# Attention over 256-key ranges with float32 scores and two query tiles per bank

## The chip, the cores and the metric

The kernel runs as one program on one core of a Trainium2 chip. The metric is the device time of one execution in microseconds, given as the median of several runs. The core has a matrix engine (TensorE, PE in the profile, with its weight loads listed as PEld), three engines for everything else (VectorE or DVE, ScalarE or ACT, GpSimd or POOL) and a queue engine (SyncE or SP) that issues most transfers. TensorE writes to PSUM, eight banks of 512 float32 columns by 128 partitions; VectorE and ScalarE read it, GpSimd doesn't.

## The reference, cut to what matters

The attention of 2 batches, 8 heads, 768 positions and 64 channels a head is followed by a mixing over the sequence, a two-layer channel mixing and a gated channel mixing. Only the attention is changed. A query sees the 8 global keys at the start and the 96 keys up to its own; the bias is the distance times a slope of the head.

```python
scores = scale * np.matmul(q, k.transpose(0, 1, 3, 2))
rel = pos[:, None] - pos[None, :]
is_global = pos[None, :] < int(n_global)                 # 8
is_local = (rel >= 0) & (rel < int(n_local))             # 96
dist = np.where(is_global & ~is_local, float(n_local), np.abs(rel))
scores = scores - slopes[:, None, None] * dist
scores = np.where(is_global | is_local, scores, -1e9)
a = np.exp(scores - scores.max(-1, keepdims=True))
attn = np.matmul(a / (a.sum(-1, keepdims=True) + 1e-9), v)
```

What follows (U and V of rank 32, then w_ch1, w_ch2, then w_k, w_v, w_r) takes the attention's output as `yp`. The weights arrive as 64-bit words and are turned into pairs of float32r parts by VectorE, ScalarE and GpSimd in the background (`conv`, lines 454 to 472).

## The kernel before, in words

**Head pairs and slots.** The 16 heads are handled as 8 pairs (`PRS`), the two heads of a pair on partitions 0 to 63 and 64 to 127. Each pair's 768 queries are 6 tiles (`NT`) of 128. `slot(pp)` lists the steps of one slot: scores and normalization of pair pp, transposes and P times V of pair pp - 1, preparation of Q and K of pair pp + 1, loads of pair pp + 2. There are 9 slots. Into some are woven steps of other work: slot 5 has the sequence mixing of batch 0 (`u_steps(0)`), slot 7 a split of its result, slot 8 the first channel products; weight conversions are woven into slots 3 and 7. A framework then schedules all instructions by priority and readiness, so the order on an engine is close to that of the lists but not the same, and each engine works its own list in order. It also puts in the waits between engines.

**One pair.** `qprep` and `kprep` transpose Q and K on TensorE and copy them out of PSUM in two float32r parts: ScalarE writes the high part, VectorE the rest (lines 272, 273, 291, 292). K is laid out as `k0 k1 g k2 k3 g k4 k5`, where `g` are the first 32 keys, copied in by VectorE (line 296), so that each query tile's window is one run of 128 to 288 columns. `score` forms three float32r products for each head and query tile (high by high, high by low, low by high), each head with 64 rows of the array and a bank of its own (line 308). VectorE adds the distance window and takes the row's minimum in one instruction (line 312); ScalarE takes the exponential and the row's sum (line 315). `norm` has GpSimd multiply by the reciprocal of the sum (line 334), and copy the 32 global columns of tiles 2 to 5 into `PN`, multiplied too (line 337). `trans` transposes 11 blocks of P for each head on TensorE, four to a bank (line 351); `tglob` transposes `PN` (line 359). These banks are emptied by `ecopy`, which gives every third copy to VectorE (line 512) and the others to ScalarE (line 510). `pv` multiplies with V, each head in a column half of the array, with up to two query tiles in a product (line 374), and adds one product of the global keys for four query tiles and both heads with `VG` (line 367). ScalarE writes the output to `yp` (lines 378 and 380).

**PSUM.** The eight banks have three names: three "a" (scores, later first-layer products), three "t" (all transposes, later half of the second-layer products), two "x" (P times V, later the other half). Line 618 is the first layer of the channel mixing, line 631 the second, lines 717, 733 and 744 the gated one.

Of the kernel before, what the change touches and what calls it, by code (L numbers as in the profile page):

```python
# [23 lines left out]
NGMAX = 32  # L24
# [8 lines left out]
def body(tc, out, q, k, v, n_global, n_local, U, V, w1, w2, mu_k, mu_r, wk, wv, wr):  # L33
    nc = tc.nc
    with ExitStack() as ctx:
# [23 lines left out]
        def constants():  # L59
# [6 lines left out]
            nc.vector.tensor_scalar(out=flag_f[:, 1:2], in0=nl[0:1], scalar1=128.0, scalar2=None, op0=ALU.is_gt)  # L66
# [87 lines left out]
        def attention_windows(pool, actx, cctx, bctx, bank, ecopy):  # L154
            pt_p = pool("ptp", 4, "right", actx)
            st_p = pool("stp", 3, "right", cctx)
            np_p = pool("npp", 11, "right", cctx)
            v_p = pool("vin", 2, "right", cctx)
            pg_p = pool("pgp", 2, "right", cctx)
# [18 lines left out]

            def load_v(pp):
                b, p = PRS[pp]  # L180
                z = st[pp]
                z["v"] = v_p.tile([128, NT, 2, D], F32, tag="vin", name="vin")
                for t in range(2):
                    nc.sync.dma_start(out=z["v"][:, :, t, :],
                                      in_=v[b, 2 * p + t].rearrange("(t p) d -> p t d", p=128))
# [6 lines left out]
            # products of zeros keep the clock of the tensor engine up until the first loads arrive  # L192
# [8 lines left out]
            # distance windows  # L201
            DW = ac.tile([128, 128 + 256 + 288 + 288], F32, name="DW")
            W0, W1, WA, WB = DW[:, 0:128], DW[:, 128:384], DW[:, 384:672], DW[:, 672:960]

            def windows():
                def scratch(dt, n, nm):
                    return np_p.tile([128, 576], dt, tag="P", name=nm)[:, 0:n]
# [15 lines left out]
                nc.vector.copy_predicated(W1, m0.bitcast(U32), relf)  # L223
# [4 lines left out]
                dg = WA[:, 128:160]  # L228
                nc.vector.copy_predicated(dg, gm.bitcast(U32), gd)
                nc.vector.tensor_copy(out=W0, in_=W1[:, 128:256])  # L230
                nc.vector.tensor_copy(out=WA[:, 0:128], in_=W1[:, 0:128])
                nc.vector.tensor_copy(out=WA[:, 160:288], in_=W1[:, 128:256])
                nc.vector.tensor_copy(out=WB[:, 0:32], in_=dg)
                nc.vector.tensor_copy(out=WB[:, 32:288], in_=W1)
                nc.vector.tensor_tensor(out=W0[:, 0:32], in0=W0[:, 0:32], in1=dg, op=ALU.min)
                nc.vector.tensor_tensor(out=W1[:, 0:32], in0=W1[:, 0:32], in1=dg, op=ALU.min)

            VG = gc.tile([64, NPR, 128], F32, name="VG")
            nc.gpsimd.memset(VG, 0.0)

            def load_vg():
                for b in range(B):
                    for t in range(2):
                        nc.sync.dma_start(
                            out=VG[32 * t:32 * (t + 1), b * NP:(b + 1) * NP, 64 * t:64 * (t + 1)],
                            in_=v[b].rearrange("(p t) s d -> t s p d", t=2)[t, 0:32])

            # columns of K: k0 k1 g k2 k3 g k4 k5; the window of a query tile is one run of them
            WIN = {0: (0, 128, W0), 1: (0, 256, W1), 2: (128, 288, WA), 3: (256, 288, WB),
                   4: (416, 288, WA), 5: (544, 288, WB)}  # L250
            # in a window: where the key tile before, the own key tile and the global keys begin
            OFF = {0: (None, 0, None), 1: (0, 128, None), 2: (0, 160, 128), 3: (32, 160, 0),
                   4: (0, 160, 128), 5: (32, 160, 0)}
# [7 lines left out]
            def qprep(pp):  # L261
                b, p = PRS[pp]
                z = st[pp]
                QS = z["QS"] = qk_p.tile([128, 2, S], F32R, tag="QS", name="QS")
                for t0, t1 in HALF:
                    ps = bank("t", "qps")
                    n = (t1 - t0) * 128
                    for i in range(t0, t1):
                        nc.tensor.transpose(ps[:, (i - t0) * 128:(i - t0 + 1) * 128],
                                            z["q"][:, i].rearrange("p h d -> p (h d)"), ident)  # L270
                    cc = slice(t0 * 128, t1 * 128)
                    nc.scalar.activation(out=QS[:, 0, cc], in_=ps[:, 0:n], func=ACTF.Copy, scale=cs[:, p:p + 1])
                    nc.vector.scalar_tensor_tensor(out=QS[:, 1, cc], in0=ps[:, 0:n], scalar=cs[:, p:p + 1],
                                                   in1=QS[:, 0, cc].bitcast(F32), op0=ALU.mult, op1=ALU.subtract)

            def kprep(pp):
# [4 lines left out]
                z["PN"] = pg_p.tile([128, 4, 2, 32], F32, tag="PN", name="PN")  # L281
                KK = z["KK"] = qk_p.tile([128, 2, 3 * 288], F32R, tag="KK", name="KK")
                KKv = KK.rearrange("p l (a n) -> p l a n", a=3)
                for t0, t1 in HALF:
                    ps = bank("t", "kps")
                    a0, a1 = t0 // 2, t1 // 2
                    for i in range(t0, t1):
                        nc.tensor.transpose(ps[:, (i - t0) * 128:(i - t0 + 1) * 128],
                                            z["k"][:, i].rearrange("p h d -> p (h d)"), ident)
                    pv = ps[:, 0:256 * (a1 - a0)].rearrange("p (a n) -> p a n", n=256)  # L290
                    nc.scalar.copy(out=KKv[:, 0, a0:a1, 0:256], in_=pv)
                    nc.vector.tensor_tensor(out=KKv[:, 1, a0:a1, 0:256], in0=pv,
                                            in1=KKv[:, 0, a0:a1, 0:256].bitcast(F32), op=ALU.subtract)
                    if t0 == 0:
                        for a in range(2):
                            nc.vector.tensor_copy(out=KKv[:, :, a, 256:288], in_=KKv[:, :, 0, 0:32].bitcast(F32))

            def score(pp, i):
                b, p = PRS[pp]
                z = st[pp]  # L300
                k0, n, W = WIN[i]
# [16 lines left out]
            def norm(pp, i0, i1):  # L318
# [4 lines left out]
                for i in range(i0, i1):  # L323
                    for t in range(2):
# [3 lines left out]
                        elif i == 1 or i % 2:  # L328
                            o = OFF[i][0]
                            Pl = Pw[:, o:o + 256]  # L330
                        else:
                            Pl = bass.AP(Pw.tensor, Pw.offset, [list(Pw.ap[0]), [160, 2], [1, 128]])
# [476 lines left out]
```

## Time and profile before

| | |
|---|---|
| median of 3 runs | 585.89 us (585.64 to 588.92) |
| profiled execution, span from first to last instruction | 584.2 us, that is 1.7 us less than the median |
| TensorE busy | 564.8 us (97%), 2830 matrix instructions |
| VectorE, ScalarE, GpSimd busy | 336.4, 245.7, 203.1 us |
| last write of attention output (line 380) | starts at 141.8 us |

A profile page gives busy times of each engine, the span in 40 slices, the chain of work that ended last (followed back from the last instruction to what released it), the costliest groups of instructions by line, and the transfers. A group's row reads: line, engine, operation, written tile and read tiles, shape, number of instructions, then busy time in us and mean ns of one, then the engine's idle time just before them and what ended most of it. A matrix product of float32 operands appears as two MATMUL instructions, one of float32r as one. Other views of the same trace show the instructions in order of time, the waits, and busy times in chosen stretches.

### The profile page before, as it was taken

To read this page: it belongs to the slowest core of one execution; us is meant where nothing else is said; L and a number is where in the kernel's file an instruction comes from. 1 tells how busy PE (TensorE), PEld (TensorE's weight loads), DVE (VectorE), ACT (ScalarE), POOL (GpSimd) and SP (SyncE) were. 2 spreads that over 40 slices of the span, in tenths; PEclk is the share of its full clock that TensorE was granted. 3 is DMA by queue.
4 is the path that set the end of the run, shared out by engine and by line. 5 is a ranking of instruction groups with operands and counts; after the bars stand their busy time and mean duration, and the time that the engine had idled before them with its cause. 6 is when DMAs were issued, how large, how long until landed. Compare 5 with 4: busy or idle time off the path is not lost.

```text
span 584.2 us, 7845 instructions
## 1 busy us (share of the span) xinstructions
PE 564.8 (97%) x2830; PEld 442.1 (76%) x2830; DVE 336.4 (58%) x737; ACT 245.7 (42%) x551; POOL 203.1 (35%) x280
## 2 busy tenths in 40 slices
PE   7899999998998999999999999999799999999996
PEld 4666765665786888888888888888688888888886
DVE  5789847896699743737272746569823352344101
ACT  4889856987454413131041332145342144124200
POOL 1577633695053402121040421154452144123300
PEclk9999999999999999999999999999989999999999
DMA  8568821133216320504021224004000000000011
GB/s 159 115 155 232 208 55 29 30 103 119 95 26 204 111 93 0 145 0 145 0 93 52 73 72 145 0 2 144 1 0 20 36 19 0 37 18 20 1 37 41
DMA packets 50031, 41.36 MB, mean 71 GB/s; under 512 B 41472, under 2 KB 41728, under 8 KB 49984
## 3 DMA queue, kind: packets, MB, share of 16 engines
q1 hardware_dynamic: 49696, 40.78, 24.2%
q8 instruction: 24, 0.39, 0.3%
q14 instruction: 23, 0.19, 0.1%
q10 hardware_dynamic: 288, 0.00, 0.0%
HBM read 37.62 MB, written 3.15 MB: 70 GB/s over the span
## 4 chain that ended last, share of the span: by engine, by line
PE 78%; DVE 13%; ACT 3%; issue 2%; POOL 2%; DMA 1%; ACTq 0%; DVEq 0%; POOLq 0%
PE aps L618 19%; PE bps L631 17%; PE pvs L744 11%; PE kps L717 10%; PE prs L733 6%; PE s L308 4%; PE tp L351 3%; DVE cvc L461 3%; PE xb L374 2%; DVE cvc L463 2%; PE gps L551 2%; DVE cvt L459 1%; POOL P L334 1%; ACT P L315 1%; DVE yp L635 1%
## 5 line engine op out<-in xcount | busy, mean ns | idle before, releaser
L618 PE MATMUL aps<-us,w1s 128*128 128x512 f32 x576 | 134.2, 390 | 2.3 <-DVE rs L622 2.3
L631 PE MATMUL bps<-rs,w2s 128*128 128x512 f32 x576 | 133.4, 389 | 0.0
L618 PEld LDWEIGHTS aps<-us,w1s 128*128 128x128 f32 x576 | 107.6, 188 | 26.9 <-DVE rs L622 3.1
L631 PEld LDWEIGHTS bps<-rs,w2s 128*128 128x128 f32 x576 | 108.1, 188 | 22.4
L621 ACT ACTIVATE rs<-aps 128x512 fp32r<-128x512 f32 x48 | 28.1, 595 | 132.6 <-PE aps L618 132.5
L717 PE MATMUL kps<-mix,wk 128*128 128x512 f32 x288 | 67.7, 396 | 3.4 <-DVE kf L722 3.4
L717 PEld LDWEIGHTS kps<-mix,wk 128*128 128x128 f32 x288 | 55.1, 192 | 15.5 <-DVE kf L722 3.9
L334 POOL TENSOR_SCALAR P<-P,sm 128x256 f32<-128x256 f32 (+1 forms) x96 | 48.9, 518 | 43.2 <-DVE sm L322 29.1
L622 DVE SCALAR_TENSOR_TENSOR rs<-aps,rs 128x512 fp32r<-128x512 f32 x48 | 32.9, 687 | 53.3 <-ACT rs L621 53.1
L744 PE MATMUL pvs<-wv,kh 128*128 128x512 f32 (+1 forms) x208 | 61.9, 373 | 0.0
L461 DVE SCALAR_TENSOR_TENSOR cvc<-cvc,cvt 128x512 uint32<-128x512 uint32 (+2 forms) x55 | 49.3, 910 | 10.0 <-ACT cvc L460 9.9
L635 DVE TENSOR_TENSOR yp<-bps,yp 128x512 f32<-128x512 f32 (+1 forms) x64 | 33.9, 550 | 31.2 <-PE bps L631 31.2
L315 ACT ACTIVATE P<-P,nm 128x288 f32<-128x288 f32 (+2 forms) x96 | 48.1, 505 | 6.2 <-DVE nm L312 5.8
L470 POOL TENSOR_TENSOR w2s<-cvc,w2s 128x512 fp32r<-128x512 f32 x16 | 24.7, 1566 | 66.8 <-ACT w2s L468 66.8
L699 POOL TENSOR_SCALAR mixt<-yp,mu 128x512 f32<-128x512 f32 (+1 forms) x32 | 21.6, 681 | 74.8 <-DVE mixf L701 30.3
L460 ACT ACTIVATE cvc<-stg 128x512 f32<-128x512 f32 (+2 forms) x55 | 36.4, 668 | 24.8 <-POOL w1s L470 6.9
L470 POOL TENSOR_TENSOR w1s<-cvc,w1s 128x512 fp32r<-128x512 f32 x16 | 22.8, 1443 | 68.2 <-ACT w1s L468 68.2
L312 DVE CUSTOM_DVE_ANT_0 P<-s,DW 128x288 f32<-128x288 f32 (+2 forms) x96 | 37.3, 417 | 13.1 <-PE s L308 12.7
L463 DVE SCALAR_TENSOR_TENSOR cvc<-stg,cvc 128x512 uint32<-128x512 uint32 (+1 forms) x54 | 43.4, 822 | 0.1
L744 PEld LDWEIGHTS pvs<-wv,kh 128*128 128x128 f32 x208 | 38.1, 188 | 6.9
L724 POOL TENSOR_TENSOR kl<-kf,kh 128x512 fp32r<-128x512 f32 x24 | 31.0, 1290 | 35.1 <-ACT kh L723 35.1
L308 PE MATMUL s<-KK,QS 64*128 64x288 f32 (+2 forms) x288 | 40.7, 323 | 1.4 <-DVE nm L312 1.1
(114 smaller groups left out, 716.6 us busy)
## 6 DMA issues: line engine op xcount, KB each, us to landing
stg<-in_moe_w_ch_dram SPq DMA_DIRECT2D x32, 512.0 KB, 4.3
stg<-in_moe_w_k_dram SPq DMA_DIRECT2D x8, 512.0 KB, 4.4
stg<-in_moe_w_v_dram SPq DMA_DIRECT2D x8, 512.0 KB, 3.8
qin<-in_q_dram SPq DMA_DIRECT2D x16, 192.0 KB, 3.5
kin<-in_k_dram SPq DMA_DIRECT2D x16, 192.0 KB, 3.6
vin<-in_v_dram SPq DMA_DIRECT2D x16, 192.0 KB, 3.3
out_dram<-sg SPq DMA_DIRECT2D x11, 256.0 KB, 2.0
stg<-in_moe_w_r_dram SPq DMA_DIRECT2D x4, 512.0 KB, 3.9
```

The source lines that it names most:

```text
L308: nc.tensor.matmul(sps[t], lhsT=z["QS"][r, lq, qs], rhs=z["KK"][r, lk, k0:k0 + n], start=(x == 0), stop=(x == 2))
L312: nc.vector.tensor_tensor_reduce(out=P[:, t, 0:n], in0=sp, in1=W, scale=2.0 ** -(2 * p + t + 1), scalar=TOP, op0=ALU.add, op1=ALU.min, acc ...
L315: nc.scalar.activation(out=P[:, t, 0:n], in_=P[:, t, 0:n], func=ACTF.Exp, scale=-1.0, bias=z["nm"][:, i, t:t + 1], accum_out=z["sm"][:, i, ...
L334: nc.gpsimd.tensor_scalar(out=Pl, in0=Pl, scalar1=sc, scalar2=1.0, op0=ALU.mult, op1=ALU.mult)
L461: nc.vector.scalar_tensor_tensor(out=c, in0=c, scalar=3, in1=t, op0=ALU.logical_shift_left, op1=ALU.bitwise_or)
L463: nc.vector.scalar_tensor_tensor(out=c if plain is None else plain, in0=Hh, scalar=0x80000000, in1=c, op0=ALU.bitwise_and, op1=ALU.bitwise_or)
L470: nc.gpsimd.tensor_tensor(out=lo, in0=f, in1=hi.bitcast(F32), op=ALU.subtract)
L618: nc.tensor.matmul(ps, lhsT=wsl(("w1", g), lw, kk, f * 128, 128), rhs=us[c][:, lx, kk, :], start=(n == 0), stop=(n == 11))
L631: nc.tensor.matmul(ps, lhsT=wsl(("w2", g), lw, f, o * 128, 128), rhs=r[:, lx, f, :], start=(n == 0), stop=(n == 11))
L635: nc.vector.tensor_tensor(out=ys, in0=ps[:, a:e], in1=ys, op=ALU.add)
L717: nc.tensor.matmul(ps, lhsT=wsl("wk", lw, kk, f * 128, 128), rhs=xk[:, lx, kk, :], start=(n == 0), stop=(n == 11))
L744: nc.tensor.matmul(pv, lhsT=ks[c][lx][:, f, t * 128:(t + 1) * 128], rhs=wsl("wv", lw, f, c0, c1 - c0), start=(n == 0), stop=(n == 23))
```

## The change

- **Key ranges.** K is laid out as six tiles of 160 columns: 128 keys and then the 32 global keys. The window of query tile i > 0 is one run of 256 columns: the last 96 keys of the tile before, the 32 global keys, the own 128 keys. Tile 0 keeps 128 columns. This serves up to 96 local keys (before: 128); beyond it the general path runs, as before.
- **A second copy of V.** `vg` holds for each query tile from 1 on the rows that belong to the first 128 columns of its window: 96 rows of V and the 32 global ones, so P times V needs two products of 128 rows for each tile and head, and no separate product of the global keys. `PN`, `PG`, `VG` and `tglob` go.
- **Scores.** Q and K are no longer split; each head and tile has one float32 product. VectorE's parts of `qprep` and `kprep` go. K leaves PSUM by `ecopy`; GpSimd copies the global columns.
- **Two query tiles per bank.** `score` handles two tiles: columns 0 to 255 and 256 to 511 of one bank for each head. There are four "a" banks and two "t" banks. In `slot` the calls of `score` are 0, 2 and 4 in place of 0 to 5, and `tglob` goes.
- **P times V** runs in blocks of 128 columns, with one "x" bank for tiles 0 and 1 and one for the other four.

The diff, cut to its core:

```diff
-            np_p = pool("npp", 11, "right", cctx)
+            np_p = pool("npp", 12, "right", cctx)
...
             def load_v(pp):
...
+                z["vg"] = v_p.tile([128, NT - 1, 2, D], F32, tag="vgin", name="vgin")
                 for t in range(2):
+                    vh = v[b, 2 * p + t]
+                    nc.sync.dma_start(out=z["v"][:, :, t, :], in_=vh.rearrange("(t p) d -> p t d", p=128))
+                    nc.sync.dma_start(out=z["vg"][0:96, :, t, :],
+                                      in_=vh[32:672].rearrange("(t p) d -> p t d", p=128)[0:96])
+                    g = vh[0:32]
+                    nc.sync.dma_start(out=z["vg"][96:128, :, t, :],
+                                      in_=bass.AP(g.tensor, g.offset, [list(g.ap[0]), [0, NT - 1], list(g.ap[1])]))
...
             def qprep(pp):
-                    nc.scalar.activation(out=QS[:, 0, cc], in_=ps[:, 0:n], func=ACTF.Copy, scale=cs[:, p:p + 1])
-                    nc.vector.scalar_tensor_tensor(out=QS[:, 1, cc], in0=ps[:, 0:n], scalar=cs[:, p:p + 1],
-                                                   in1=QS[:, 0, cc].bitcast(F32), op0=ALU.mult, op1=ALU.subtract)
+                    nc.scalar.activation(out=QS[:, t0 * 128:t1 * 128], in_=ps[:, 0:n], func=ACTF.Copy,
+                                         scale=cs[:, p:p + 1])
             def kprep(pp):
-                    nc.scalar.copy(out=KKv[:, 0, a0:a1, 0:256], in_=pv)
-                    nc.vector.tensor_tensor(out=KKv[:, 1, a0:a1, 0:256], in0=pv,
-                                            in1=KKv[:, 0, a0:a1, 0:256].bitcast(F32), op=ALU.subtract)
+                    ecopy(out=KKv[:, t0:t1, 0:128], in_=pv)
                     if t0 == 0:
-                        for a in range(2):
-                            nc.vector.tensor_copy(out=KKv[:, :, a, 256:288], in_=KKv[:, :, 0, 0:32].bitcast(F32))
+                        nc.gpsimd.tensor_copy(out=KKv[:, 0:NT - 1, 128:KS],
+                                              in_=KKv[:, 0:1, 0:32].to_broadcast([128, NT - 1, 32]))
+            def score(pp, i0):
+                sps = [bank("a", "s") for t in range(2)]
+                for x in range(2):
+                    i = i0 + x
+                    k0, n = (KS * (i - 1) + 32, 256) if i else (0, 128)
+                    for t in range(2):
+                        r = slice(64 * t, 64 * (t + 1))
+                        nc.tensor.matmul(sps[t][:, 256 * x:256 * x + n], lhsT=z["QS"][r, i * 128:(i + 1) * 128],
+                                         rhs=z["KK"][r, k0:k0 + n], start=True, stop=True)
+                for x in range(2):
...
             def norm(pp, i0, i1):
+                        Pl = z["P"][i][:, t, 0:256 if i else 128]
-                        if i >= 2:
-                            o = OFF[i][2]
-                            nc.gpsimd.tensor_scalar(out=z["PN"][:, i - 2, t, :], in0=Pw[:, o:o + 32], scalar1=sc,
-                                                    scalar2=1.0, op0=ALU.mult, op1=ALU.mult)
             def pv(pp, half):
+                X = bank("x", "xa" if half == 0 else "xb")
+                i0, i1 = ((0, 2), (2, NT))[half]
+                for i in range(i0, i1):
+                    for x in (0,) if i == 0 else (2 * i - 1, 2 * i):
+                        for t in range(2):
+                            lhsT = z["vg"][:, i - 1, t, :] if x % 2 else z["v"][:, i, t, :]
+                            nc.tensor.matmul(X[64 * t:64 * (t + 1), c0:c0 + 128], lhsT=lhsT, rhs=z["PT", t][:, x, :],
+                                             start=(x == (0, 3)[half]), stop=(x == (2, 10)[half]))
             def slot(pp):
...
                 add(cur, score, pp, 4)
+                add(cur, norm, pp, 3, 6)
                 add(pre, trans, o, 0, 2)
-                add(cur, score, pp, 5)
-                add(cur, norm, pp, 3, 6)
                 add(pre, trans, o, 1, 2)
...
-                banks = {"a": 3, "t": 3, "x": 2}
+                banks = {"a": 4, "t": 2, "x": 2}
```

More of the change, by code (lines that the diff above doesn't have):

```diff
@@ L227, in windows @@
                 nc.vector.tensor_scalar(out=gd, in0=colf, scalar1=0.0, scalar2=nl, op0=ALU.mult, op1=ALU.add)
-                dg = WA[:, 128:160]
+                dg = W1[:, 96:128]
                 nc.vector.copy_predicated(dg, gm.bitcast(U32), gd)
                 nc.vector.tensor_copy(out=W0, in_=W1[:, 128:256])
[L231 to L234, printed above, removed]
                 nc.vector.tensor_tensor(out=W0[:, 0:32], in0=W0[:, 0:32], in1=dg, op=ALU.min)
[L236 to L253, printed above, removed]
+            KS = 160
             HALF = ((0, 4), (4, 6))
@@ L263, in qprep @@
                 z = st[pp]
-                QS = z["QS"] = qk_p.tile([128, 2, S], F32R, tag="QS", name="QS")
+                QS = z["QS"] = qk_p.tile([128, S], F32, tag="QS", name="QS")
                 for t0, t1 in HALF:
@@ L300, in score @@
                 z = st[pp]
-                k0, n, W = WIN[i]
-                P = z["P"][i] = np_p.tile([128, 2, 288], F32, tag="P", name="P")
-                qs = slice(i * 128, (i + 1) * 128)
-                sps = [bank("a", "s")[:, 0:n] for t in range(2)]
-                for t, x in ((0, 0), (0, 1), (1, 0), (0, 2), (1, 1), (1, 2)):
-                    lq, lk = ((0, 0), (0, 1), (1, 0))[x]
-                    r = slice(64 * t, 64 * (t + 1))
-                    nc.tensor.matmul(sps[t], lhsT=z["QS"][r, lq, qs], rhs=z["KK"][r, lk, k0:k0 + n],
-                                     start=(x == 0), stop=(x == 2))
@@ L348, in trans @@
                 ps = bank("t", "tp").rearrange("p (a n) -> p a n", a=4)
-                for x, (j, i) in enumerate(blks):
-                    o = OFF[i][1] if i == j else OFF[i][0]
-                    nc.tensor.transpose(ps[:, x, :], z["P"][i][:, t, o:o + 128], ident)
+                for x, (i, c) in enumerate(blks):
+                    nc.tensor.transpose(ps[:, x, :], z["P"][i][:, t, c:c + 128], ident)
                 ecopy(out=z["PT", t][:, 4 * g:4 * g + m, :], in_=ps[:, 0:m, :])
-            def tglob(pp):
-                z = st[pp]
-                z["PG"] = pg_p.tile([64, 4, 128], F32, tag="PG", name="PG")
-                ps = bank("t", "tg").rearrange("p (a n) -> p a n", a=4)
-                for x in range(4):
-                    nc.tensor.transpose(ps[0:64, x, :], z["PN"][:, x].rearrange("p h c -> p (h c)"), ident)
-                ecopy(out=z["PG"], in_=ps[0:64])
             def pv(pp, half):
@@ L393, in slot @@
                 add(pre, trans, o, 0, 0)
-                add(cur, score, pp, 1)
                 add(pre, trans, o, 1, 0)
@@ L399, in slot @@
                 add(pre, trans, o, 0, 1)
-                add(cur, score, pp, 3)
                 add(pre, trans, o, 1, 1)
-                add(pre, tglob, o)
                 add(nxt, kprep, pp + 1)
```

77 lines of the change are left out of this document (26 added, 51 removed).

## The prediction

> **What bounds the kernel now.** I read the page first.
>
> ```profile
> span 584.2 us, 7845 instructions
> PE 564.8 (97%) x2830; PEld 442.1 (76%) x2830; DVE 336.4 (58%) x737; ACT 245.7 (42%) x551; POOL 203.1 (35%) x280
> PE 78%; DVE 13%; ACT 3%; issue 2%; POOL 2%; DMA 1%; ACTq 0%; DVEq 0%; POOLq 0%
> ```
>
> The execution profiled has a span of 584.2 us; the median of the runs is 585.89, so 1.7 us lie around it. TensorE is busy 97% and is 78% of the chain that ended last. The change touches only the attention, so the table by stretch comes next, cut where the output rows of a head pair (`yp<-xb`) are written, which ends a slot. A row has the stretch and its length, the busy time and instructions of PE, PEld, DVE, ACT and POOL, the granted clock, the DMA share and GB/s.
>
> ```profile
> 11.00:35.30 24.30, 22.01 (x157) 15.25 (x158) 16.76 (x79) 19.69 (x65) 13.15 (x35) 1.00 0.60 126
> 35.30:48.60 13.30, 12.83 (x107) 9.27 (x106) 12.21 (x44) 12.96 (x40) 7.84 (x17) 1.00 0.81 209
> 48.60:63.00 14.40, 14.11 (x106) 10.02 (x105) 13.50 (x47) 12.25 (x38) 10.59 (x22) 1.00 0.75 206
> 63.00:75.70 12.70, 12.63 (x104) 8.94 (x103) 9.47 (x39) 11.16 (x36) 8.74 (x22) 1.00 0.70 178
> 75.70:102.70 27.00, 27.00 (x158) 15.33 (x159) 17.37 (x49) 17.53 (x48) 9.32 (x24) 1.00 0.20 45
> 102.70:116.20 13.50, 13.40 (x100) 9.08 (x99) 11.52 (x42) 12.19 (x38) 8.86 (x19) 1.00 0.13 30
> 116.20:129.40 13.20, 12.64 (x92) 8.69 (x91) 12.38 (x40) 12.20 (x37) 13.02 (x23) 1.00 0.38 109
> 129.40:142.40 13.00, 12.30 (x83) 9.23 (x82) 8.34 (x11) 8.97 (x19) 10.48 (x15) 1.00 0.27 84
> ```
>
> Each slot is as long as TensorE is busy in it, to 0.7 us. But in the five slots of 12.7 to 14.4 us ScalarE stands between 0.1 us ahead of it and 1.9 behind. So TensorE time saved counts only until ScalarE is the longer one; that sets the sum. (The stretch at 75.7 holds the first half of the mixing too.)
>
> **TensorE, per slot.** The timeline of the slot from 63 us, PE only, start and length first. Matmul lengths hold the pipeline's tail, so I take start to next start.
>
> ```profile
> 63.35 0.62 PE L308 MATMUL s<-KK,QS 64*128 64x256 f32 x6
> 63.91 0.66 PE L351 MATMUL tp<-ident,P 128*128 128x128 f32 x4
> ...
> 65.15 0.67 PE L308 MATMUL s<-KK,QS 64*128 64x288 f32 x6
> 65.75 0.66 PE L351 MATMUL tp<-ident,P 128*128 128x128 f32 x4
> ...
> 67.94 0.39 PE L308 MATMUL s<-KK,QS 64*128 64x288 f32 x1
> 68.26 0.63 PE L359 MATMUL tg<-ident,PN 128*64 128x128 f32 x4
> 68.72 0.82 PE L288 MATMUL kps<-ident,kin 128*128 128x128 f32 x6
> ...
> 71.04 1.02 PE L367 MATMUL xb<-PG,VG 64*128 64x512 f32 x2
> 71.99 0.55 PE L351 MATMUL tp<-ident,P 128*128 128x128 f32 x3
> 72.47 0.87 PE L374 MATMUL xa<-PT,vin 128*64 128x256 f32 x8
> 73.17 1.90 PE L374 MATMUL xb<-PT,vin 128*64 128x128 f32 x20
> 75.00 0.44 PE L542 MATMUL xtp<-ident,yp 128*128 128x128 f32 x2
> ```
>
> *Global keys.* The transposes tg (0.46 us, 68.26 to 68.72) and the product with VG (0.95) go: 1.41 us.
>
> *P times V.* The list shows one float32 product of VG as two MATMULs (x2). The 20 of xb are 12 of 256 columns and 8 of 128: 4096 columns in 1.83 us, 0.45 ns each. VG's two need 0.95 us for 1024 columns, 0.93 ns each. So the two heads of P times V, in two halves of the array, run at once. After the change there are 11 blocks of 128 columns, the same 1408 columns for each head, in 44 MATMULs instead of 28: 44 x 128 x 0.45 = 2.53 us, as now (0.70 + 1.83). Finer pieces: 0 to +0.4 us; I take 0.
>
> *Scores.* Now 6 float32r products per query tile, three for each head: 0.56 us at 256 columns, 0.60 at 288. A tile that finds too few of the three banks "a" is torn: the one product at 67.94 holds TensorE 0.32 us.
>
> ```profile
> L308 PE MATMUL s<-KK,QS 64*128 64x288 f32 (+2 forms) x288 | 40.7, 323 | 1.4 <-DVE nm L312 1.1 <-DVE KK L292 0.3
> ```
>
> 40.7 / 8 = 5.1 us per slot, tails in; less 0.07 for some seven runs, 4.6. After: three calls of two tiles. Float32 at 64 rows in two row halves isn't in the trace. The nearest rows: float32 in column halves runs at once, and so does float32r in row halves: at 0.45 ns per column (134.2 us for 576 of 512 columns in L618, quoted below) 6 x 256 would need 0.70 us in turn and took 0.56 with fill and drain. If the new ones do too, a call is 8 MATMULs of 256 columns at 0.45, 0.92 us, plus 0.21 to fill and drain (0.56 less 3 x 256 x 0.45): 1.13, and 0.90 for the call with tile 0. That is 3.2 us per slot, 1.4 less than now. If they don't, 0.93 ns a column gives 2.1 + 2.1 + 1.6 = 5.8, 1.2 more. I take the first.
>
> The Trainium skill, "TensorE: Matmul & The Clock Gate", section The mechanism, says that MATMULs keep strict order in start and end and only weight loads are pulled ahead. By it the second pass of one head would run beside the first of the other, and each call would end one pass later than I take; the rivals price this from rows.
>
> TensorE thus loses 1.4 + 1.4 = 2.8 us per slot, 22 over eight pairs. That is the ceiling.
>
> **ScalarE, VectorE, GpSimd.** Groups up to 142.4 us:
>
> ```profile
> L315 ACT ACTIVATE P<-P,nm 128x288 f32<-128x288 f32 (+2 forms) x96 | 48.1, 505 | 6.2 <-DVE nm L312 5.8
> L291 ACT CAST KK<-kps 128x512 fp32r<-128x512 f32 (+1 forms) x16 | 7.0, 479 | 1.3 <-PE kps L288 1.1
> L510 ACT COPY PG<-tg 64x512 f32<-64x512 f32 x5 | 2.9, 575 | 0.3 <-PE tg L359 0.3
> L273 DVE SCALAR_TENSOR_TENSOR QS<-qps,cs,QS 128x512 fp32r<-128x512 f32 (+1 forms) x16 | 9.2, 611 | 0.1
> L292 DVE TENSOR_TENSOR KK<-kps,KK 128x512 fp32r<-128x512 f32 (+1 forms) x16 | 8.1, 548 | 0.0
> L296 DVE CAST KK<-KK 128x64 fp32r<-128x64 f32 x16 | 2.4, 190 | 0.0
> L337 POOL TENSOR_SCALAR PN<-P,sm 128x32 f32<-128x32 f32 x64 | 23.5, 367 | 0.0
> ```
>
> ScalarE keeps all 96 exponentials (32 columns fewer in 64 of them, 0.15 us per slot as an estimate), loses a third of the K copies (7.0 / 8 / 3 = 0.29) and PG (2.9 / 8 = 0.36): **0.8 us per slot**, of 11 to 13. VectorE loses (9.2 + 8.1 + 2.4) / 8 = 2.5 us and takes 0.4 of K copies. GpSimd loses 2.9 and gains one copy of 160 columns per pair; nearest row: 367 ns for 32 columns, so 0.37 and somewhat more. That copy stands in GpSimd's queue behind up to three tiles of P multiplies, and the next pair's scores wait for it; K is transposed at 68.72, 6.3 us before the slot's products are done (75.00), which hides it; without that cover up to 2 us a slot.
>
> **Transfers.** A pair issues six loads instead of two; the four of VG go.
>
> ```profile
> vin<-in_v_dram SPq DMA_DIRECT2D x16, 192.0 KB, 3.3
> q1 hardware_dynamic: 49696, 40.78, 24.2%
> ```
>
> 24.2% of 584 us over 49,696 packets is 2.8 ns each over the 16 engines; 1280 more small packets make 3.6 us of transfer per pair. Beside a share of 0.81 that fills the engines in the slots at 35 to 75 us, but V is used a slot after its issue, and Q and K of a pair more than half a slot after theirs: hidden. If not, 1 to 2 us in each of three slots.
>
> **Banks.** "t" goes from 3 to 2 and now holds ten groups a slot (six of P, two Q, two K).
>
> ```profile
> 66.60 0.69 DVE L512 COPY PT<-tp 128x512 f32<-128x512 f32 x1
> 67.34 0.42 PEld L351 LDWEIGHTS tp<-ident,P 128*128 128x128 f32 x4 [0.31 <-DVE PT L512]
> ```
>
> The group at 65.75 holds its bank until 67.29, 1.54 us, and with three banks TensorE already waited 0.31 us for one. Ten groups at 1.6 to 1.8 over two banks are 8 to 9 us of a slot: below ScalarE, but close enough to add waits. Later work uses "t" and "x" in turn:
>
> ```profile
> L618 PE MATMUL aps<-us,w1s 128*128 128x512 f32 x576 | 134.2, 390 | 2.3 <-DVE rs L622 2.3
> L631 PE MATMUL bps<-rs,w2s 128*128 128x512 f32 x576 | 133.4, 389 | 0.0
> ```
>
> A group of 12 takes 2.8 us (134.2 / 48), and a "t" bank returns after three or more groups, so L631 stays without a wait; the fourth "a" bank can win back at most L618's 2.3 us. I take 0 for the rest after 142.4 us and shift it.
>
> **The sum.** A slot after is the larger of TensorE less 2.8 and ScalarE less 0.8, plus 0.7 for two engines of nearly one length (today up to 0.7 over TensorE). At 35.3: 12.2 + 0.7 against 13.3, saves 0.4. At 48.6: 11.5 + 0.7 against 14.4, 2.2. At 63.0: 10.4 + 0.7 against 12.7, 1.6. At 75.7 TensorE stays longest: 24.2 + 0.3 against 27.0, 2.5. At 102.7: 11.4 + 0.7, 1.4. At 116.2: 11.4 + 0.7, 1.1. The last has no scores; tg and VG go, 1.3. From 11 to 35.3 ScalarE is nearly full from 12 us on, 1.6 from it and 0.4 at the end: 2.0. The start loses the low parts of Q and K and four window copies on VectorE but still waits for the limits from memory: 0.5 of a possible 2.5. Sum 13.0: 585.9 - 13.0 = **573 us**.
>
> **Rivals.** *TensorE's whole saving counts* (the order written by the framework fills ScalarE's idle time, 24 of 131 us in the rows above): 22 us and 1 at the start, 563. For it: PE leads the chain; against: ScalarE's 12.96 of 13.30.
> *The row halves don't run at once:* scores +1.2 for 1.4 saved: 0.2 us in each of seven slots, the last slot's 1.3 and the start: 583, no change to measure. Against it: the 0.56 of a 256-column tile.
> *Strict order of MATMULs:* two passes of one head come ahead of the other's, so each call ends a pass (0.24 us) later; 24 calls, 6 us: 579. Against it: the float32r products stand in the code with two of one head in a row, which would give four steps of 0.12 and 0.21, 0.69 us, not 0.56. This is the rule of the Trainium skill's "TensorE: Matmul & The Clock Gate" named above; the trace doesn't bear it out.
> *Slower: the two "t" banks.* Evictions on ScalarE queue behind exponentials of 0.5 us each. Once a group holds its bank over 2.66 us on the mean (10 x 2.66 / 2 = 13.3), the banks set the slot. If each eviction came three exponentials later (3 x 0.505), 3.0 us each, the slot would be 15, +1.7 in seven slots: 598. Against it: 1.54 now, and VectorE, which evicts one in three, loses work.
>
> **How the numbers follow.** Forecast 0.62 (568 to 579); whole saving 0.14; no overlap 0.08; strict order 0.06; banks 0.10, of it half inside 1%. A measurement of this kernel tells about 1%, 5.9 us, from no change. Faster: 0.62 + 0.14 + 0.06 = 0.82, less 0.02 for the forecast's edge: 0.80. Same: 0.08 + 0.05 + 0.02 = 0.15. Slower 0.05. The range takes in the whole saving at 563 and the lack of overlap at 583, with 1 us on either side for V's loads, pieces and banks.
>
> **What would show it.** Right: s falls from 40.7 to about 27 us and x288 to x192; L359, L367, L337, L273, L296 are gone; `yp<-xb` is last written at about 130 us; ScalarE is busy over 90% of the slots and stands in the chain where PE stood; the rest after it keeps its 442 us (584.2 less 142.4). Wrong: s near 45; idle of tp put down to PT copies over 10 us; scores waiting for GpSimd's copy into KK or for DMA; a longer stretch after the attention.

## The result and the profile after

The changed kernel takes **572.08 us** (median of 4 runs, 571.46 to 572.15), against 586.62 us for the kernel before in the same job: ratio 0.973, 95% interval 0.9696 to 0.9763. The profiled execution has a span of 570.2 us, 14.0 less than the 584.2 of before. The prediction was 573.0 in a range of 562 to 584.

The total is right, but its two halves are not where the prediction put them. The last head pair's rows are now written at 132.8 us instead of 142.35, so the attention gave 9.6 us and not 13.0. The rest takes 437.4 us (570.2 less 132.8) instead of 441.8, so 4.4 us came from code that the diff doesn't touch and that the prediction left at zero. The last of these copies on the timelines of before and after (start, length):

```profile
141.76 0.59 ACT L380 COPY yp<-xb 128x512 f32<-128x512 f32 x1
```
```profile
132.20 0.58 ACT L342 COPY yp<-xb 128x512 f32<-128x512 f32 x1
```

The page of the changed kernel: span, share of each engine, the chain that ended last, and the groups of the later products (the line; busy time, mean ns; idle time before them and what ended it).

```profile
span 570.2 us, 7710 instructions
PE 549.4 (96%) x2814; PEld 430.7 (76%) x2814; DVE 318.0 (56%) x688; ACT 238.5 (42%) x540; POOL 184.6 (32%) x223
...
PE 79%; DVE 9%; ACT 4%; POOL 2%; issue 2%; SPq 1%; DMA 1%; POOLq 0%; DVEq 0%
...
L576 PE MATMUL aps<-us,w1s 128*128 128x512 f32 x576 | 135.1, 391 | 0.4 <-DVE rs L580 0.4
...
L675 PE MATMUL kps<-mix,wk 128*128 128x512 f32 x288 | 65.8, 389 | 0.0
```

TensorE is still what bounds the kernel, and ScalarE didn't take its place in the chain. The stretches of the attention, cut again where `yp<-xb` is written (length; busy time and instructions of PE, PEld, DVE, ACT, POOL; granted clock, DMA share, GB/s):

```profile
0.00:30.75 30.75, 24.65 (x173) 15.58 (x174) 16.67 (x95) 20.75 (x68) 12.08 (x34) 1.00 0.77 151
30.75:42.20 11.45, 11.45 (x102) 8.15 (x102) 5.23 (x26) 9.96 (x32) 5.10 (x13) 1.00 0.59 133
42.20:54.70 12.50, 12.11 (x104) 8.28 (x102) 6.84 (x32) 10.05 (x34) 5.95 (x15) 1.00 0.78 185
54.70:68.80 14.10, 12.54 (x105) 9.32 (x104) 9.90 (x39) 11.52 (x38) 7.27 (x15) 1.00 0.49 110
68.80:97.80 29.00, 27.75 (x167) 15.18 (x165) 17.04 (x65) 21.57 (x65) 8.80 (x19) 1.00 0.40 107
97.80:109.70 11.90, 10.39 (x94) 7.40 (x92) 10.44 (x29) 9.36 (x26) 10.54 (x14) 1.00 0.53 150
109.70:120.70 11.00, 9.81 (x86) 6.85 (x87) 9.43 (x32) 10.28 (x32) 7.14 (x9) 1.00 0.79 209
120.70:132.80 12.10, 10.94 (x91) 8.87 (x89) 11.86 (x17) 9.09 (x18) 9.18 (x10) 1.00 0.41 134
```

ScalarE is busy for less time than TensorE in seven of the eight, and for over 90% of the stretch in one of them only, where the prediction expected it of the slots. Against before, the first stretch became 4.5 us shorter and five of the slots 0.9 to 2.2 each, but the slot that ends at 68.8 grew by 1.4 and the one that ends at 97.8 by 2.0.

**Where the other 4.4 us are.** The page of before has, in its list of groups, a row that the prediction never looked at:

```profile
L717 PE MATMUL kps<-mix,wk 128*128 128x512 f32 x288 | 67.7, 396 | 3.4 <-DVE kf L722 3.4
```

That is the gated mixing. From its first product to the first of `prs` the stretch of before, and three pieces of it cut at the steps of the granted clock:

```profile
410.20:437.40 27.20, 23.76 (x98) 19.14 (x98) 14.74 (x21) 11.01 (x19) 13.76 (x11) 0.94 0.00 1
416.41:419.83 3.42, 2.17 (x10) 1.48 (x8) 3.42 (x5) 0.62 (x1) 1.51 (x2) 1.00 0.00 0
419.83:423.24 3.41, 1.22 (x5) 1.04 (x6) 1.04 (x3) 2.24 (x4) 1.81 (x2) 1.00 0.00 0
423.24:426.65 3.41, 3.41 (x9) 2.65 (x9) 1.30 (x2) 1.79 (x4) 2.23 (x3) 0.50 0.00 0
```

and the same stretch of the changed kernel:

```profile
401.10:422.90 21.80, 21.80 (x98) 18.02 (x97) 13.51 (x19) 9.68 (x17) 13.19 (x10) 1.00 0.00 1
```

With three "a" banks TensorE had filled all three and waited 3.44 us for VectorE's `kf`; then the clock stood at 0.50 for 3.41 us, which costs half of these 3.41 us, 1.7, on top. With four banks there is neither: 27.1 us became 21.8, **5.3 us** won. L618's wait of 2.3 us is 0.4 now too (L576 above), another 1.9. Of these 7.2 us some 2.8 are given back elsewhere between 132.8 us and the end, 1.7 of them in longer waits of TensorE in the sequence mixing (L509) and before L589.

### The profile page after: what moved, and what is told of

Same layout as the page of the kernel before. It is cut to its first block, busy times and chain, and to the rows that moved or that the text cites. A ratio compares the mean times of both kernels' runs of the same rounds, so it can differ in the third digit from the quotient of the medians.

```text
span 570.2 us, 7710 instructions
## 1 busy us (share of the span) xinstructions
PE 549.4 (96%) x2814; PEld 430.7 (76%) x2814; DVE 318.0 (56%) x688; ACT 238.5 (42%) x540; POOL 184.6 (32%) x223
## 4 chain that ended last, share of the span: by engine, by line
PE 79%; DVE 9%; ACT 4%; POOL 2%; issue 2%; SPq 1%; DMA 1%; POOLq 0%; DVEq 0%
PE aps L576 19%; PE bps L589 19%; PE pvs L702 12%; PE kps L675 11%; PE prs L691 6%; PE s L292 3%; ACT P L302 2%; PE tp L327 2%; PE gps L509 2%; PE xb L340 2%; POOL P L313 2%; DVE cvc L419 2%; DVE cvc L421 2%; DVE us L547 1%; DVE cvt L417 1%
## 5 line engine op out<-in xcount | busy, mean ns | idle before, releaser
L576 PE MATMUL aps<-us,w1s 128*128 128x512 f32 x576 | 135.1, 391 | 0.4 <-DVE rs L580 0.4
L589 PE MATMUL bps<-rs,w2s 128*128 128x512 f32 x576 | 133.8, 389 | 0.8 <-DVE yp L593 0.8
L576 PEld LDWEIGHTS aps<-us,w1s 128*128 128x128 f32 x576 | 107.5, 188 | 25.2 <-issue 2.5
L589 PEld LDWEIGHTS bps<-rs,w2s 128*128 128x128 f32 x576 | 107.9, 188 | 23.5 <-PE bps L589 1.2
L675 PE MATMUL kps<-mix,wk 128*128 128x512 f32 x288 | 65.8, 389 | 0.0
L313 POOL TENSOR_SCALAR P<-P,sm 128x256 f32<-128x256 f32 (+1 forms) x96 | 50.4, 546 | 35.3 <-DVE sm L309 20.5
L419 DVE SCALAR_TENSOR_TENSOR cvc<-cvc,cvt 128x512 uint32<-128x512 uint32 (+2 forms) x55 | 46.2, 852 | 7.2 <-ACT cvc L418 6.8
L302 ACT ACTIVATE P<-P,nm 128x256 f32<-128x256 f32 (+1 forms) x96 | 46.2, 485 | 8.7 <-DVE nm L299 8.5
L421 DVE SCALAR_TENSOR_TENSOR cvc<-stg,cvc 128x512 uint32<-128x512 uint32 (+1 forms) x54 | 47.1, 892 | 0.1
L299 DVE CUSTOM_DVE_ANT_0 P<-s,DW 128x256 f32<-128x256 f32 (+1 forms) x96 | 34.0, 396 | 18.9 <-PE s L292 18.7
L702 PE MATMUL pvs<-wv,kl 128*128 128x512 f32 (+1 forms) x104 | 38.8, 373 | 0.0
```

The source lines that it names most:

```text
L299: nc.vector.tensor_tensor_reduce(out=P[:, t, 0:n], in0=sps[t][:, 256 * x:256 * x + n], in1=W, scale=2.0 ** -(2 * p + t + 1), scalar=TOP, o ...
L302: nc.scalar.activation(out=P[:, t, 0:n], in_=P[:, t, 0:n], func=ACTF.Exp, scale=-1.0, bias=z["nm"][:, i, t:t + 1], accum_out=z["sm"][:, i, ...
L313: nc.gpsimd.tensor_scalar(out=Pl, in0=Pl, scalar1=z["sm"][:, i, t:t + 1], scalar2=1.0, op0=ALU.mult, op1=ALU.mult)
L419: nc.vector.scalar_tensor_tensor(out=c, in0=c, scalar=3, in1=t, op0=ALU.logical_shift_left, op1=ALU.bitwise_or)
L421: nc.vector.scalar_tensor_tensor(out=c if plain is None else plain, in0=Hh, scalar=0x80000000, in1=c, op0=ALU.bitwise_and, op1=ALU.bitwise_or)
L576: nc.tensor.matmul(ps, lhsT=wsl(("w1", g), lw, kk, f * 128, 128), rhs=us[c][:, lx, kk, :], start=(n == 0), stop=(n == 11))
```

## The experiments

**One part undone: the banks.** Two kernels, each with the other's banks: the changed kernel with three "a" and three "t", and the kernel before with four and two.

```diff
-banks = {"a": 4, "t": 2, "x": 2}     # in the changed kernel
+banks = {"a": 3, "t": 3, "x": 2}
```

> The changed kernel with the banks of before, three "a" and three "t". Theory: the wait for kf returns, 27 us from the first kps<-mix product to the first prs product, 5.3 us more; in the attention three "a" banks tear more score calls of two tiles (TensorE +1 to +4 us) and the third "t" bank takes away the waits of transposes for ScalarE's copies (5 us in all in the waits), so the attention ends within 2 us of 132.8 and the time is 575 to 580. Rival 1 (the banks do nothing later): 570 to 573. Rival 2 (two "t" banks hold the attention back): it ends 4 us earlier.

> The kernel before with four "a" and two "t" banks, nothing else. Theory (a fourth bank carries TensorE over the first products of the gated mixing): the wait of L717 for kf, 3.4 us before, goes and with it the halved clock behind it, so the stretch from the first kps<-mix product to the first prs product falls from 27.1 to 21.8 us, 5.3 less, and the time by 3 to 6 us, since two "t" banks may cost up to 2 in the attention. Rival (the 5.3 us came from the order of the later work having shifted, not from the banks): that stretch stays at 27 us and the time within 2 us of 586.

The changed kernel with the old banks: 581.11 us, ratio to before 0.9896 (0.9847 to 0.9945), so 9 us are lost and the time lies 1 us above the theory's range. The page's row of `kps` and the last stretch have the old wait back; the two stretches ahead of it have the clock halved:

```profile
L675 PE MATMUL kps<-mix,wk 128*128 128x512 f32 x288 | 67.7, 396 | 3.4 <-DVE kf L680 3.4
```
```profile
119.17:126.00 6.83, 5.39 (x16) 4.45 (x17) 2.52 (x6) 1.78 (x4) 2.62 (x3) 0.50 0.45 142
136.24:139.65 3.41, 3.41 (x10) 2.66 (x9) 2.33 (x6) 0.91 (x2) 3.41 (x1) 0.50 0.77 184
403.60:430.70 27.10, 23.70 (x98) 19.08 (x96) 14.64 (x21) 10.92 (x19) 13.74 (x11) 0.94 0.00 1
```

Its attention ended at 131.3, 1.5 us earlier than with two "t" banks although the clock was halved for 6.83 us in it: the new banks do cost the attention something, and pay it back later. Behind the attention the profiled execution is 9.1 us longer: 5.3 in the mixing, 1.9 in L576's waits, some 1.7 of the clock halved at 136.24. The kernel before with the new banks: 599.62 us, ratio 1.0204 (1.0157 to 1.0251), not the 3 to 6 us less that were expected. Its mixing took 21.75 us as foreseen, but the attention ended at 160.2, 17.8 later. Of these, 10.6 lie behind 109.8 us, and this is why (the waits, then the stretch in which nothing ran on TensorE, the one behind it, and the mixing):

```profile
ACT cvc L460 <- POOL w1s L470: 6.8, 1, 6.8
```
```profile
126.70:130.10 3.40, 0.00 (x0) 0.00 (x0) 0.61 (x4) 0.78 (x2) 2.58 (x5) 1.00 0.86 325
130.15:147.21 17.06, 15.84 (x68) 9.60 (x69) 6.57 (x23) 9.55 (x32) 7.37 (x20) 0.50 0.13 43
429.75:451.50 21.75, 21.75 (x97) 18.02 (x96) 13.46 (x19) 9.67 (x17) 13.17 (x10) 1.00 0.00 1
```

ScalarE's next instruction was a weight conversion's copy, and its buffer was held by an earlier conversion whose low part stood in GpSimd's queue. ScalarE, and with it its evictions of "t" banks, stood for 6.8 us; TensorE emptied; the clock then ran at half for 17 us. The other 7.2 us were lost earlier, 0.7 to 2.6 in each stretch. The first of these holds 10.2 us of halved clock; no wait of TensorE between 36 and 110 us is longer than 0.7 us, and the cause stays open. So the new banks help the later stages alone, and whether they help the sum depends on the rest. That the wait for `kf` hangs on the banks is shown by all 14 traces: it is there, 3.39 to 3.44 us long, in the eight kernels with three "a" banks and in none of the six with four.

**One part undone: the scores.** The changed kernel with its Q and K split again and three float32r products; two query tiles in a bank as they are.

```diff
-nc.tensor.matmul(sps[t][...], lhsT=z["QS"][r, ...], rhs=z["KK"][r, ...], start=True, stop=True)
+for t, m in ((0, 0), (0, 1), (1, 0), (0, 2), (1, 1), (1, 2)):   # three products per head, low parts on VectorE
```

> The changed kernel with the scores alone undone: Q and K split again by ScalarE and VectorE and three float32r products for each head and tile; key ranges, second V and two tiles per bank stay. TensorE then streams 3 x 256 columns where the float32 product streams 4 x 256, so a call of two tiles should take 0.87 us instead of 1.06, 24 calls 4.6 us less; VectorE gets 2.2 us a slot more, ScalarE 0.3. Theory that TensorE's length sets the slots: 568 to 570. Theory that copies out of PSUM and the two "t" banks set them (VectorE holds Q's and K's banks 1.1 us longer per pair): 572 to 578. Theory of the change's own words (unsplit products are what pays): 577 or more.

584.65 us, ratio 0.9957 (0.9939 to 0.9976): 12.6 us of the gain are gone, which only the third theory allowed, and the attention ends 13.6 later. The middle slots stayed within 1.3 us of what they were; the start lost 6.4 and the last two 6.9. The first stretch, and two pieces of it with the clock halved:

```profile
0.00:37.10 37.10, 29.43 (x200) 20.99 (x200) 20.49 (x101) 21.57 (x67) 13.24 (x38) 0.82 0.63 130
9.64:16.46 6.82, 6.57 (x40) 5.47 (x42) 2.58 (x12) 3.46 (x12) 0.64 (x2) 0.50 0.69 138
19.88:26.70 6.82, 5.00 (x29) 4.15 (x30) 3.08 (x18) 5.28 (x21) 4.46 (x12) 0.50 0.69 135
```

TensorE or VectorE? The next kernel keeps the float32 scores and lets VectorE compute the low parts all the same.

```diff
+ql = qk_p.tile([128, 512], F32R, tag="QL", name="QL")
+nc.vector.scalar_tensor_tensor(out=ql[:, 0:n], in0=ps[:, 0:n], scalar=cs[:, p:p + 1],
+                               in1=QS[:, cc], op0=ALU.mult, op1=ALU.subtract)   # and the like for K
```

> The changed kernel, scores in float32 as they are, but VectorE still computes the low parts of Q and K as before (they are not used), so that the transposes' banks are held for them too. Theory A, the 12.6 us that the changed kernel loses when its scores go back to three float32r products come from VectorE's 2.2 us a slot and the two banks held longer: 579 to 586. Theory B, they come from TensorE's products: 572 to 576.

578.60 us, ratio 0.9841 (0.9799 to 0.9884), between the two theories: 6.5 of the 12.6 us come back with VectorE's split and the banks held for it. (K's copies all go to ScalarE then, which also shifts the turns in which the engines copy P, so the split doesn't stand quite alone.) It is not the slots that pay but the two ends (stretches, then TensorE's waits in the last one):

```profile
0.00:34.50 34.50, 26.39 (x180) 16.46 (x180) 21.79 (x109) 23.07 (x76) 12.96 (x36) 1.00 0.71 140
122.25:139.10 16.85, 12.31 (x88) 9.26 (x86) 13.89 (x20) 8.70 (x18) 10.41 (x11) 0.90 0.40 127
```
```profile
PE aps L581 <- POOL w1s L433: 1.9, 1, 1.9
PE tp L332 <- POOL P L318: 1.6, 1, 1.6
```

At the start, where little else is there to run, the split stands between Q's and K's transposes and the first scores: 34.5 us instead of 30.75. In the last slot there is no split; there the order has shifted, TensorE waits twice for GpSimd, and 3.4 us of halved clock follow: 16.85 instead of 12.1. The float32r kernel's attention ends another 7.3 us later: 2.7 of it at the start, 2.0 in the next five slots, 2.6 in the last two. There the longer products and the halved clock can't be told apart.

**One part alone: float32 scores in the kernel before**, one product per head and tile, everything else as it was; and the same with the seven early weight conversions one to a slot, beside the kernel before with its conversions so spread, since the first had met the stall shown above.

```diff
-for t, x in ((0, 0), (0, 1), (1, 0), (0, 2), (1, 1), (1, 2)):   # three float32r products
+for t in range(2):                                              # one float32 product
```
```diff
-CONV = {3: 3, 7: 4}
+CONV = {1: 1, 2: 1, 3: 1, 4: 1, 5: 1, 6: 1, 7: 1}
```

> The kernel before with one part of the change alone: Q and K unsplit, the scores as one float32 product per head and query tile (windows of 288, three and three banks, the global products and V's pieces stay as they were). Theory A, the scores are the larger part of the gain whatever else changes: TensorE needs about 0.5 us for a tile instead of 0.60 (-0.7 us a slot) and VectorE loses 2.3 us a slot, so the attention ends 6 to 11 us earlier than 142.4 and the time is 575 to 580. Theory B, float32 scores pay only with two query tiles in a bank: one tile's product of 2 x 288 columns with its fill and drain and the change between float32 and transposes leaves it where it was, 584 to 588.

> The kernel before, the seven conversions of weights that stand in slots 3 and 7 put one to a slot (slots 1 to 7), nothing else: the yardstick for the next runs, in which no copy of a conversion on ScalarE should stand for long behind a conversion's low part that waits in GpSimd's queue, as it did for 5.5 us with float32 scores alone and for 4.8 us with finer pieces alone. Theory A, before had no such stall (1.0 us), so this is its equal: 584 to 588. Theory B, the place of the conversions is worth some us of itself: 578 to 583.

> Float32 scores alone in the kernel before, conversions one to a slot. Theory A, the 6 us by which float32 scores alone were slower than before came from the stall of a conversion and the halved clock behind it, and the scores themselves gain: 5 to 9 us under the run with conversions spread alone, 577 to 582. Theory B, the scores gain only with two tiles to a bank: within 2 us of it.

Alone: 591.77 us, ratio 1.0058 (1.0036 to 1.0081), a little slower and above both expectations. ScalarE had stood for 5.5 us (the waits), TensorE for a whole stretch, and the clock fell:

```profile
ACT cvc L454 <- POOL uv L466: 5.5, 1, 5.5
```
```profile
62.50:65.90 3.40, 0.00 (x0) 0.00 (x0) 0.45 (x1) 0.27 (x1) 3.01 (x7) 1.00 0.49 162
65.92:72.74 6.82, 5.16 (x19) 2.95 (x20) 3.10 (x12) 5.53 (x18) 0.00 (x0) 0.50 0.47 115
```

Spread alone is worth nothing measurable (587.43; 0.9971, 0.9943 to 0.9999). Float32 scores on top of it: 589.01 (1.001, 0.998 to 1.004). That kernel still met a stall of 4.5 us, with the clock halved for 6.83 us behind it, so it isn't clean either, but the 577 to 582 of theory A are far off, and its products show why. The waits of the float32 kernel, then the groups of `s` up to the attention's end, spread alone and with float32 scores, then two runs from the latter's timeline:

```profile
ACT cvc L454 <- POOL w1s L464: 4.5, 1, 4.5
```
```profile
L308 PE MATMUL s<-KK,QS 64*128 64x288 f32 (+2 forms) x288 | 40.0, 321 | 2.2 <-DVE nm L312 1.9 <-DVE KK L292 0.3
```
```profile
L303 PE MATMUL s<-KK,QS 64*128 64x288 f32 (+2 forms) x192 | 42.4, 437 | 1.1 <-ACT KK L289 0.6 <-DVE nm L306 0.5
```
```profile
35.42 0.76 PE L303 MATMUL s<-KK,QS 64*128 64x288 f32 x4
...
39.53 0.75 PE L303 MATMUL s<-KK,QS 64*128 64x288 f32 x2
```

The product of one head (x2) takes as long as those of both (x4), since the second half of the array would have run beside it; 15 of the 50 runs of `s` hold one head alone. And a whole tile isn't cheaper either: from start to next start its four MATMULs hold TensorE for 0.69 us (the middle of 29 such runs), where six float32r products held it for 0.60. In the changed kernel a call of two tiles holds it for 1.06 us, 0.53 a tile of 256 columns. VectorE's relief is there in both float32 kernels (the first head pair's rows are written at 33.25 us instead of 35.44 with the conversions spread), but the slots behind give it back. So the theory that float32 alone is the larger part of the gain fell, as far as two disturbed runs can tell: it pays with two tiles to a bank, not by itself.

**The global keys' way and the pieces.** P times V in pieces of 128 columns in the kernel before; and that with the global keys' own transposes and product left out, with the conversions as they were and spread.

```diff
-runs = ((0, 0, 2), (1, 2, 3), (1, 3, 4), (2, 4, 6), (3, 6, 8), (4, 8, 10), (5, 10, 11))
+runs = tuple((j, x, x + 1) for x, (j, i) in enumerate(BLK))
```
```diff
-add(pre, tglob, o)                 # and the PN multiplies, and the product with VG
```

> The kernel before with P times V in pieces of 128 columns (44 MATMULs a pair instead of 28), as the second copy of V needs them, nothing else. Theory A, the pieces cost what the two traces suggest, 0.4 us a slot: attention 3 us later, 589 to 591. Theory B, the prediction's term: pieces are free, 586 to 588.

> The same with pieces of 128 columns, and the global keys' own way left out: no 32-column multiplies on GpSimd, no tg transposes, no PG copy, no product with VG (the output lacks the contribution of the global keys to query tiles 2 to 5). Against the run with pieces alone: theory A, TensorE binds and its 1.41 us a slot all counts: 10 to 13 us less, 576 to 580. Theory B, the prediction's rule, ScalarE becomes the longer engine and only its 0.4 us of PG a slot counts: 3 to 4 us less, 584 to 587.

> The kernel before with P times V in pieces of 128 columns and the global keys' own way left out (the output lacks the contribution of the global keys to query tiles 2 to 5), conversions one to a slot. Theory A, TensorE binds: 1.41 us a slot for the global keys less 0.4 for the pieces, some 8 us under the run with conversions spread alone: 575 to 580. Theory B, ScalarE binds: 3 us under it, 581 to 585.

Pieces alone: 600.82 us, ratio 1.0189 (1.0132 to 1.0246). Both expectations missed it; there is the stall again, and the clock is halved for 13.65 us twice, the first time without a stall (the waits, then the two stretches):

```profile
ACT cvc L460 <- POOL w1s L470: 4.8, 1, 4.8
```
```profile
10.92:24.57 13.65, 13.38 (x62) 10.55 (x62) 7.79 (x35) 8.22 (x27) 3.09 (x8) 0.50 0.63 133
...
130.38:144.04 13.66, 12.88 (x73) 8.97 (x74) 6.40 (x21) 7.86 (x27) 7.38 (x18) 0.50 0.24 72
```

As a price of pieces it is of no use, nor as a yardstick. Without the global way: 584.20 (0.9892, 0.982 to 0.9963), and spread 578.10 (0.9823, 0.9773 to 0.9873). Against the spread kernel's 587.43 the last is **9.3 us** less, more than the 3 that ScalarE's bound would allow and about the 8 of TensorE's. (Its profile, of the slowest of six executions, has 17 us at half clock at the start.) GpSimd's multiplies are gone in it as well, but TensorE's waits for GpSimd in the spread kernel are 1.4 us in all, so they can't be most of it. So TensorE bound most of those slots; in the last three it is busy without a break in both kernels, as in the second row:

```profile
11.47:28.54 17.07, 16.92 (x79) 12.89 (x77) 9.86 (x48) 12.13 (x41) 5.26 (x12) 0.50 0.56 116
...
116.40:126.60 10.20, 10.20 (x103) 7.96 (x102) 9.65 (x37) 8.91 (x31) 7.76 (x13) 1.00 0.37 94
```

**Is ScalarE the bound of the changed kernel?** Every second copy of a transposed tile to VectorE instead of every third.

```diff
-if RR[0] % 3:
+if RR[0] % 2:
```

> The changed kernel with every second copy of ecopy on VectorE instead of every third: ScalarE loses 1.3 of its 8 copies a slot, 0.7 us, VectorE gains 0.9. If ScalarE sets the slots now: 3 to 6 us less, 566 to 569. If TensorE does: within 1.5 us of 572.

575.24 us, ratio 0.9801 (0.9753 to 0.985): 3 us slower than the changed kernel and outside both expectations. The two ends lost, the first stretch 1.4 us and the last 2.8, with TensorE waiting there for GpSimd (the last stretch, then a wait in it):

```profile
120.01:134.90 14.89, 11.94 (x93) 8.64 (x91) 12.53 (x17) 8.71 (x17) 10.38 (x12) 1.00 0.39 122
```
```profile
PE aps L576 <- POOL w1s L428: 1.4, 2, 1.0
```

But the six slots between them became 2.1 us shorter in sum. So ScalarE's copies do count for something in the slots, about 0.35 us each, and less than the 3 to 6 us that the prediction's rule would have given: ScalarE alone doesn't set them. Whether the ends lost by VectorE's added copies or by a shifted order isn't shown.

**Could the two longer slots be had back?** The changed kernel with the conversions one to a slot.

> The changed kernel, the seven conversions one to a slot. Theory A, the two slots at 54.6 to 97.8 that came out longer than predicted did so because the conversions of slots 3 and 7 landed there together: 568 to 571, the attention ended 1 to 4 us before 132.8. Theory B, ScalarE and TensorE have the same work in sum and nothing is won: 571 to 573.

575.06 us, ratio 0.9766 (0.9718 to 0.9813), again 3 us slower and outside both expectations. The conversions moved, and in the first of the two slots another wait opened: TensorE's transposes behind ScalarE's copy of Q, with two "t" banks (the waits, then the stretch and the one behind it).

```profile
PE tp L327 <- ACT QS L261: 3.8, 1, 3.8
```
```profile
61.85:65.26 3.41, 0.81 (x7) 0.81 (x8) 1.63 (x4) 3.01 (x11) 3.33 (x5) 1.00 0.56 136
65.26:72.09 6.83, 6.74 (x35) 4.22 (x33) 1.25 (x2) 1.91 (x4) 2.65 (x7) 0.50 0.27 60
```

So the run decides nothing on the first slot, and the second stayed as long as it was (28.9 us). The changed kernel's own trace says more. In the slot that ends at 68.8 the same wait stands for 1.3 us, most of the 1.4 by which it grew (in us: in total, times, the longest, which is this one):

```profile
PE tp L327 <- ACT QS L261: 1.7, 2, 1.3
```

The slot that ends at 97.8 holds 46 of the 192 MATMULs of the scores, nearly two head pairs' worth (24 each); before, it held 45 of 288, one pair and a quarter. The slot behind it has 10 now, and had 33. So at least part of its length is work that the order has moved forward out of slots that became shorter. No variant beat the changed kernel.

## Why the prediction was right in sum and wrong in parts

Per slot below is an eighth of the time from a matmul's start to the next one's, over the attention of each trace; TensorE's idle time is named beside it.

**Global keys, -1.41 us a slot on TensorE: right, a little small.** In before the product with VG held TensorE for 8.1 us, the transposes `tg` for 4.4 and 1.05 of idle: 1.69 a slot. The run without them gained 9.3 us with the pieces paid and GpSimd's part of the work gone.

**Pieces, 0 (at most +0.4): too low, at the upper end of what was allowed.** P times V took 23.3 us before and takes 26.5 now, +0.4 a slot; with the conversions spread and the global way left out it was 22.7 and 26.4. What in a finer piece costs this isn't shown. Another 2.3 us, 0.3 a slot, are idle time behind the last of these matmuls; they ended at ScalarE's copies of Q and P, so they belong to the "t" banks.

**Scores, -1.4: right mechanism, wrong size.** The row halves do run at once: a run of four is as long as a run of two. A call takes 1.06 us, as against the 1.13 taken. But 10 runs hold one head alone, and pay 0.63 us for half the work:

```profile
33.56 0.70 PE L292 MATMUL s<-KK,QS 64*128 64x256 f32 x4
...
35.27 0.70 PE L292 MATMUL s<-KK,QS 64*128 64x256 f32 x2
```

36.96 us became 31.41, 0.7 a slot, and 0.4 with the idle time in and behind them. Why these runs are torn isn't shown: with three "a" banks in place of four there are 10 of them as well. The prediction took off the torn runs of before (0.07 us) and priced none after. The group's busy time shows it, 33.3 us where 27 were announced:

```profile
L292 PE MATMUL s<-KK,QS 64*128 64x256 f32 (+1 forms) x192 | 33.3, 396 | 1.9 <-POOL KK L280 1.0 <-ACT KK L468 0.9
```

The rival of the strict order, from the rule in the Trainium skill's "TensorE: Matmul & The Clock Gate", section The mechanism, is out too: by it, with the two passes of one head ahead of the other's, four would take longer than two, but the run of four and the run of two above both take 0.70 us. The trace doesn't show in which order the passes stand in the queue, so this speaks against the rival and not against the rule.

**ScalarE becomes the longer engine: wrong.** This is the step that failed. ScalarE lost about what was said (0.95 us a slot, 0.8 predicted), but TensorE lost 1.4 us a slot instead of 2.8 (1.69 for the global keys, 0.4 for the scores, less 0.7 for P times V, idle time included) and stayed the longer one in seven of the eight stretches. Copies moved off ScalarE won 2.1 us in six slots, not the 3 to 6 of the rule. The slots behind the first stretch gave 5.0 us in sum where the rule gave 10.5, and two grew.

**The start, -0.5 of a possible 2.5, and -2.0 behind it: too small.** The first stretch became 4.5 us shorter. VectorE's split stood on its path; putting the split back, with K's copies on ScalarE, cost 3.7 us there (34.5 less 30.75). "VectorE loses 2.5 us" had been counted, and then not used.

**GpSimd's copy into KK and V's second loads, 0: right for the most part.** The scores waited 1.0 us once for the copy (`POOL KK L280` in the row above); among the waits of up to 132.8 us none is for `vin` or `vgin`, though the DMA queue's share rose from 24.2%:

```profile
q1 hardware_dynamic: 59872, 43.27, 26.7%
```

No run took away what hides the copy.

**Banks, 0 in the attention: too low, and small by luck of the order.** TensorE's transposes waited 1.7 us for `QS` and some 2 us for copies of P, and with the old banks the attention ended 1.5 us earlier. In the kernel before, the new banks cost 17.8 us of attention, most of it by a stall and the halved clock behind it.

**The fourth "a" bank, 0: wrong by 7.2 us,** 1.9 at L618 and 5.3 in the gated mixing. It was weighed against L618's 2.3 us alone. L717's 3.4 us stood on the same page, in the same tag of banks, 270 us behind the change.

The two errors, 3.4 us too much for the attention and 4.4 too little for the rest, cancelled to within 1 us, which is luck. The parts also don't add: float32 scores alone are worth nothing in the old kernel and 12.6 us in the new one; the banks alone cost 12 us in the one and save 9 in the other. In the runs behind these figures the clock was halved for 14 to 27 us (last section), and every variant shifts the framework's order too; how much of the differences is due to that isn't shown. For the scores' 12.6 us it leaves open how VectorE's split and TensorE's products share them.

## What to carry to other kernels

When a change touches a pool of buffers, list every group that draws on that pool, in all stages, and read the idle time before each; the largest may lie hundreds of microseconds from the edit. Price two half-array products by what one alone costs, and count how often only one will start. A variant that leaves TensorE empty for some two microseconds pays again in a halved clock (3.4 us of it or more in every such stretch of these traces), so one part tried alone is a fair test only if its trace shows the clock unbroken.

## What the runs showed of the hardware

The granted clock falls in whole steps of 3.41 us, and on less idle time than one such step. Laid as a grid from each trace's first clock record, the stretches of 3.41 us at full clock up to 565 us in the 14 traces divide so by TensorE's idle time in them (no matmul listed):

```
idle in the stretch    stretches    followed by clock 0.50
under 0.75 us             2127               0
0.75 to 1.5                 71               3
1.5 to 1.95                 20               7
over 1.95                   16              16
```

The halved clock then lasted 3.41 to 17.1 us. The Trainium skill, "TensorE: Matmul & The Clock Gate", section HAM oscillation — how this bites in real kernels, gives as its rule that idle gaps of over about 3.4 us are to be avoided. The length of the step agrees; the gap needed here is shorter: a single one of 1.93 us, at 132.9 us of the changed kernel with the old banks, was enough, and over 1.95 us of idle in a stretch the clock was always halved behind it. (Matmul ends are modelled in the profile, so the idle times are approximate.) The grid starts at another time in each execution (3.8 to 6.9 us), so where a gap lies on the grid differs from one execution to the next; one of 1.5 to 2 us may or may not cost a step.
